# QK-normalised attention with a maxout feed-forward layer: the values' bound by a product with ones, SyncE's order by hand, weighted sums a slot later

## The chip, the cores and the metric

The kernel runs on one core of one Trainium2 chip. The metric is the device time in microseconds of one execution; lower is better. The compute engines are TensorE (PE in the profile, its weight loads PEld), VectorE (DVE), ScalarE (ACT) and GpSimd (POOL). SyncE (SP) issues every DMA of this kernel from one queue, in order.

## The reference

```python
# q, k, v: (8, 12, 448, 64)   g_q, g_k: (64,)
q_n = q / sqrt(mean(q*q, -1) + 1e-6) * g_q        # k_n likewise with g_k
scores = matmul(q_n, k_n^T) / sqrt(64)
attn = exp(scores - max(scores)); attn = attn / (sum(attn) + 1e-9)
x = matmul(attn, v)                               # heads side by side: (3584, 768)
h = maximum(maximum(x @ w1, x @ w2), x @ w3)      # each w: (768, 768) float64
out = h @ w_out                                   # float32 (3584, 768)
```

The four weight matrices come in as float64 and are decoded to float32 by integer operations on the chip. Products run at nearly float32 accuracy: queries, keys, attention weights and values are split into a float16 head and a float16 remainder, feed-forward operands into two float32r parts, and three of the four cross products are summed.

## The kernel before, in words

Work goes by pairs of heads, 48 pairs (8 batches of 6); a pair is `g`. Its life is spread over several turns of the main loop:

- Three pairs ahead, `load_k` and `load_q` fetch rows. `load_kv` uses four DMAs for a pair: for each of the two heads the first 384 rows, three to a partition, and the last 64 on one half of the partitions. The rows lie in one of three fixed tiles, of which a strip was set to zero once.
- Two pairs ahead, `squares`, `inv_rms` and `scale_k` or `scale_q` normalise the rows (VectorE sums, GpSimd raises to the power -0.5 and multiplies).
- One pair ahead, `turn_k` and `turn_q` (both through `turn_rows`) split them into float16 parts (cast L251 on ScalarE, remainder L252 on GpSimd) and turn them with one DMA transpose each (L256). The parts' tiles `kp` and `qp` have two buffers. `load_v` fetches the values and `bound_v` finds a bound for their size: VectorE takes the largest magnitude of each partition (`most`), SyncE writes these 128 numbers to DRAM (`vscr`, L276) and reads them back to all partitions (`every`, L278), and `prep_v` reduces them to one number and splits the values by it (`vp`).
- In its own turn the pair's queries come in four chunks of 112. `scores` runs six matmuls per chunk into a two-bank tile `sc` of PSUM (two buffers). `softmax` takes the negated row maximum (L326), scales it (L327) and runs the exponential with its row sum (L333). `weights` turns the sum into a factor (L343, L347), makes the float16 head (L350, ScalarE) and remainder (L351, VectorE) of the weights, and turns both with a DMA transpose into `pt` (L357).
- One pair later, `add_values` sums the weighted values in seven steps; step 3 (L372) is for the two half blocks of 64 keys, the others are at L378. `fold` brings a head's sum to its place, `finish` splits it for the feed-forward part.

The feed-forward part of a batch is a generator, `ffn`, taken in thirds. A third is three matmuls. Layer 1 (L439) has 18 units of six thirds, one per weight block; `split_w` casts and splits the block of the next unit (L112 on ScalarE, L113 on GpSimd) at a unit's second third, and `fetch` (L415, tile `wf`, two buffers) loads the block of the unit after that at its third. Layer 2 (L483) has 42 thirds on the mean and loads nothing. The decoding of the weights (`prep_w`: load `raw`, five VectorE instructions, store to DRAM as `wscr`; `prep_wo` likewise for `w_out`, kept on chip) goes beside the first nine pairs, by the table `DECODES`.

A turn of the main loop has eight slots, `i` = 0 to 7. In each slot three thirds of the feed-forward part are taken (a fourth when two batches wait). Scores of chunks 0 and 1 stand in slot 0, of chunks 2 and 3 in slot 4; the weights of the four chunks in slots 1, 2, 5 and 6; the seven steps of the weighted sums of the pair before in slots 1 to 7.

What sets the order: only TensorE's instructions stay in the order of the program text. All other queues, SyncE's included, are ordered by a planner that models the run when the program is built; at run time each queue is worked off in order, and a waiting instruction holds all behind it.

```python
ctx.enter_context(tc.manual_schedule(engines={mybir.EngineType.PE}))
```

Of the kernel before, what the change touches and what calls it, by code (L numbers as in the profile page):

```python
# [7 lines left out]
F32 = mybir.dt.float32  # L8
# [9 lines left out]
P = 128  # L18
# [18 lines left out]
def qknorm_attention_maxout_ffn_kernel(  # L37
# [60 lines left out]
    HALVES = (slice(0, 64), slice(64, 128))  # L98

    kv_rows = {}  # L100
    for name in ("kr", "vr"):
        kv_rows[name] = [const.tile([P, 2, 4, D], F32, name=f"{name}{i}") for i in range(3)]
        for t in kv_rows[name]:
            nc.gpsimd.memset(t[HALVES[1], 0, 3], 0.0)
            nc.gpsimd.memset(t[HALVES[0], 1, 0], 0.0)

# [68 lines left out]

    def load_kv(g, name, src):
        b, pr = divmod(g, NP)
        t = kv_rows[name][g % 3]
        for h in range(2):
            rows = src[b, 2 * pr + h]  # L180
            nc.sync.dma_start(
                out=t[:, h, h:h + 3],
                in_=rows[0:3 * P].rearrange("(p c) d -> p c d", c=3),
            )
            nc.sync.dma_start(out=t[HALVES[h], h, 3 - 3 * h], in_=rows[3 * P:S])
        st.setdefault(g, {})[name] = t
# [8 lines left out]
    def squares(g, what):  # L195
        s = st[g]
        src, rows = (s["kr"], P) if what == "k" else (s["qr"], QP)
        src = src.rearrange("p h c d -> p (h c) d")
        sq = sb.tile([P, 8, D], F32, name="sq", tag="rows", bufs=2)
        if g < EARLY:  # L200
            nc.scalar.activation(sq[:rows], src, AF.Square)
        else:
            nc.gpsimd.tensor_tensor(out=sq[:rows], in0=src, in1=src, op=ALU.mult)
        s["sq"] = sq[:rows]

    def inv_rms(g):
        s = st[g]
        sq = s.pop("sq")
        rows = sq.shape[0]
        ss = sb.tile([P, 8], F32, name="ss", tag="ss", bufs=2)  # L210
        nc.vector.tensor_reduce(ss[:rows], sq, axis=AX, op=ALU.add)
        nc.vector.tensor_scalar(  # L212
            out=ss[:rows], in0=ss[:rows], scalar1=1.0 / D / QK_UP ** 2,
            scalar2=RMS_EPS / QK_UP ** 2, op0=ALU.mult, op1=ALU.add,
        )
        ri = sb.tile([P, 8], F32, name="ri", tag="ri", bufs=2)
        nc.gpsimd.tensor_tensor(  # L217
            out=ri[:rows], in0=ss[:rows], in1=half_neg[:rows], op=ALU.pow
        )
        s["ri"] = ri  # L220

    def scale_rows(g, what, rows):
        s = st[g]
        r, ri = s.pop(what + "r"), s.pop("ri")
        n = sb.tile([rows, 4, 2, D], F32, name=what + "n", tag="rows", bufs=2)
        nc.gpsimd.tensor_tensor(
            out=n.rearrange("p c h d -> p h c d"),
            in0=r,
            in1=ri[:rows].rearrange("p (h c o) -> p h c o", h=2, o=1).broadcast_to([rows, 2, 4, D]),
            op=ALU.mult,  # L230
        )
        s[what + "n"] = n

    def scale_q(g):
        scale_rows(g, "q", QP)
        n = st[g]["qn"].rearrange("p c h d -> p (c h) d")
# [4 lines left out]
        )  # L241

    def scale_k(g):
        scale_rows(g, "k", P)


    def turn_rows(g, what, rows):
        s = st[g]
        n = s.pop(what + "n").rearrange("p c h d -> p (c h d)")
        parts = sb.tile([rows, 2, 4 * P], F16, name=what + "p", bufs=2)  # L250
# [3 lines left out]
        )  # L254
        t = sb.tile([P, 2, 4, rows], F16, name=what + "t", bufs=2)
# [6 lines left out]
    def turn_q(g):  # L262
        turn_rows(g, "q", QP)

    def turn_k(g):
        turn_rows(g, "k", P)


    def bound_v(g):
        s = st[g]  # L270
        most = sb.tile([P, 1], F32, name="most", bufs=2)
        nc.vector.tensor_reduce(
            most, s["vr"].rearrange("p h c d -> p (h c d)"), axis=AX, op=ALU.max, apply_absolute_value=True
        )
# [3 lines left out]
        nc.sync.dma_start(  # L278
            out=every, in_=scr.rearrange("(o p) -> o p", o=1).broadcast_to([P, P])
        )  # L280
        s["every"] = every


    def prep_v(g):
        s = st[g]
        vr, every = s.pop("vr").rearrange("p h c d -> p (h c) d"), s.pop("every")
# [11 lines left out]
        vp = sb.tile([P, 8, 2, D], F16, name="vp", bufs=2)  # L298
# [11 lines left out]
    def scores(g, chunks):  # L310
        s = st[g]
        qt, kt = s["qs"], s["ks"].rearrange("p a c r -> p a (c r)")
        for c in chunks:
            sc = ps_s.tile([P, 2, 512], F32, name="sc", tag="s")
            for n, (qp, kp) in enumerate(TERMS):
# [5 lines left out]
            s["sc", c] = sc  # L321

    def softmax(g, c):
        sc = st[g].pop(("sc", c))
        nm = sb.tile([QP, 2], F32, name="nm", bufs=3)
# [228 lines left out]
    for g in range(2):  # L554
# [3 lines left out]
        if g == 0:  # L558
            turn_k(0)
# [103 lines left out]
```

## Time and profile before

| | |
|---|---|
| median of 3 runs | 1873.96 us (1869.73 to 1875.49) |
| the profiled execution | 1879.87 us, span of its instructions 1878.1 us |
| mean granted TensorE clock | 0.804 of full |
| DMA | 513958 packets, 231.80 MB, mean 123 GB/s |
| TensorE matmuls / VectorE / ScalarE / GpSimd instructions | 5520 / 1952 / 1760 / 726 |

The profile is of one execution. In its rows, `out<-in` names the tiles, `x` a count; `<-` behind idle time names what ended it. A duration next to a transfer is from its issue to its landing. SPq is SyncE's own queue.

### The profile page before, as it was taken

What the parts mean: (1) busy time and instruction counts of PE and PEld (TensorE: products, weight loads), DVE (VectorE), ACT (ScalarE), POOL (GpSimd) and SP (SyncE); (2) the same over time, 40 slices, a digit from 0 to 9 for tenths busy, and PEclk for the clock granted to TensorE, in tenths of its full rate; (3) what the DMA queues carried; (4) which work ended last, traced back from release to release, by engine and by line L of the source; (5) the groups of instructions that cost most, each with busy time, mean ns of one, the idle gap of its engine ahead of it and who ended that gap; (6) DMA issues with size and microseconds to landing.
All of it is one profiled execution on the core that took longest, in us unless ns stands there. A gap on an engine that the chain in (4) does not pass through costs nothing. (4 is left out here: it accounts for less than half of the span.)

```text
span 1878.1 us, 18561 instructions
## 1 busy us (share of the span) xinstructions
PE 1140.2 (61%) x5520; PEld 860.2 (46%) x5520; DVE 1185.7 (63%) x1952; ACT 873.7 (47%) x1760; POOL 982.3 (52%) x726
## 2 busy tenths in 40 slices
PE   1013214646675775677567666666767667678898
PEld 0001102424453554455455454545555445566798
DVE  4667879957665765677566676567675677466310
ACT  2334334445454544454544454554544555456331
POOL 5344445656644664466555575366655566334252
PEclk9966556869788787788778777887878778788999
DMA  7979867665546545666755664754856663555431
GB/s 119 171 152 148 175 159 156 138 121 114 126 91 145 126 95 117 119 124 107 133 122 106 128 134 93 130 130 95 159 110 116 132 128 90 119 123 129 94 103 58
DMA packets 513958, 231.80 MB, mean 123 GB/s; under 512 B 433472, under 2 KB 488768, under 8 KB 513856
## 3 DMA queue, kind: packets, MB, share of 16 engines
q1 hardware_dynamic: 513856, 230.60, 60.1%
q8 instruction: 44, 0.72, 0.2%
q14 instruction: 58, 0.48, 0.1%
HBM read 111.74 MB, written 18.11 MB: 69 GB/s over the span
## 5 line engine op out<-in xcount | busy, mean ns | idle before, releaser
L439 PE MATMUL acc<-xt,wt 128*128 128x448 f32 x2592 | 689.6, 412 | 158.9 <-ACT wt L112 102.5
L439 PEld LDWEIGHTS acc<-xt,wt 128*128 128x128 f32 x2592 | 533.1, 209 | 269.6 <-ACT wt L112 113.2
L351 DVE SCALAR_TENSOR_TENSOR pp<-p,rs,pp 112x448 f16<-112x448 f32 x384 | 421.9, 1134 | 249.1 <-ACT pp L350 236.9
L333 ACT ACTIVATE p<-sc,nm,down 112x448 f32<-112x448 f32 x384 | 273.9, 721 | 313.3 <-DVE nm L327 284.3
L378 PE MATMUL av<-pt,vp 128*128 128x448 f16 x576 | 181.8, 410 | 385.8 <-DMA pt<-pp 272.8
L113 POOL TENSOR_TENSOR wt<-wf,wt 128x768 fp32r<-128x768 f32 x144 | 272.0, 1889 | 232.3 <-ACT wt L112 231.3
L217 POOL TENSOR_TENSOR ri<-ss,half_neg 128x8 f32<-128x8 f32 x96 | 175.0, 1823 | 199.9 <-DVE ss L212 172.0
L350 ACT ACTIVATE pp<-p,rs 112x448 f16<-112x448 f32 x384 | 233.0, 663 | 58.8 <-issue 39.6
L378 PEld LDWEIGHTS <-vp 128*128 128x128 f16 x576 | 38.6, 105 | 461.0 <-issue 329.2
L483 PE MATMUL acc<-wo_sb,ht 128*128 128x384 f32 x864 | 200.4, 382 | 66.3 <-ACT osb L488 35.0
L317 PE MATMUL sc<-kt,qt 64*112 64x448 f16 x1152 | 157.7, 411 | 121.9 <-ACT p L333 91.3
L252 POOL TENSOR_TENSOR kp<-kn,kp 128x512 f16<-128x512 f32 x48 | 59.4, 1237 | 318.2 <-ACT kp L251 294.9
L483 PEld LDWEIGHTS acc<-wo_sb,ht 128*128 128x128 f32 x864 | 171.1, 212 | 85.0 <-ACT osb L488 37.3
L326 DVE TENSOR_REDUCE nm<-sc 112x2 f32<-112x896 f32 x192 | 204.5, 1078 | 4.1 <-PE sc L317 2.7
L112 ACT CAST wt<-wf 128x768 fp32r<-128x768 f32 x144 | 119.6, 831 | 128.3 <-PE acc L439 59.3
L317 PEld LDWEIGHTS <-qt 64*112 64x112 f16 x1152 | 85.4, 146 | 179.1 <-issue 102.3
L343 DVE TENSOR_SCALAR sm<-sm 112x2 f32<-112x2 f32 x192 | 72.5, 378 | 130.0 <-ACT p L333 129.7
L453 DVE TENSOR_TENSOR m<-acc,m 128x448 f32<-128x448 f32 x96 | 59.0, 615 | 114.8 <-PE acc L439 114.6
L251 ACT CAST kp<-kn 128x512 f16<-128x512 f32 x48 | 29.6, 616 | 195.6 <-DMA kt<-kp 191.2
L391 DVE SCALAR_TENSOR_TENSOR x<-av,vscale,x 64x448 f32<-64x448 f32 x96 | 65.2, 679 | 53.9 <-ACT x L390 52.6
L327 DVE TENSOR_SCALAR nm<-nm,down 112x2 f32<-112x2 f32 x192 | 90.8, 488 | 0.3
L390 ACT ACTIVATE x<-av,vscale 64x448 f32<-64x448 f32 x96 | 60.4, 630 | 56.6 <-PE av L372 49.5
(55 smaller groups left out, 1204.8 us busy)
## 6 DMA issues: line engine op xcount, KB each, us to landing
wf<-wscr SPq DMA_DIRECT2D x144, 384.0 KB, 3.8
raw<-in_moe_w_dram SPq DMA_DIRECT2D x18, 768.0 KB, 6.8
qr<-in_q_dram SPq DMA_DIRECT2D x48, 224.0 KB, 3.5
kr<-in_k_dram SPq DMA_DIRECT2D x96, 96.0 KB, 4.0
vr<-in_v_dram SPq DMA_DIRECT2D x96, 96.0 KB, 2.5
wscr<-d_f SPq DMA_DIRECT2D x18, 384.0 KB, 3.6
raw<-in_moe_w_out_dram SPq DMA_DIRECT2D x6, 768.0 KB, 5.5
every<-vscr SPq DMA_DIRECT2D x48, 64.0 KB, 4.9
```

Source lines behind the costliest of these rows:

```text
L112: nc.scalar.copy(dst_hi, src)
L113: nc.gpsimd.tensor_tensor(out=dst_lo, in0=src, in1=dst_hi.bitcast(F32), op=ALU.subtract)
L217: nc.gpsimd.tensor_tensor(out=ri[:rows], in0=ss[:rows], in1=half_neg[:rows], op=ALU.pow)
L317: nc.tensor.matmul(sc[:QP, h, :S], qt[rows, qp, c], kt[rows, kp, KEYS[h]], start=n == 0, stop=n == len(TERMS) - 1,)
L326: nc.vector.tensor_reduce(nm, sc[:QP, :, :S], axis=AX, op=ALU.max, negate=True)
L327: nc.vector.tensor_scalar(out=nm, in0=nm, scalar1=down[:QP], scalar2=None, op0=ALU.mult)
L333: nc.scalar.activation(p[:, h], sc[:QP, h, :S], AF.Exp, bias=nm[:, h:h + 1], scale=down[:QP], accum_out=sm[:, h:h + 1],)
L350: nc.scalar.activation(pp[:, 0, h], p[:, h], AF.Copy, scale=rs[:, h:h + 1])
L351: nc.vector.scalar_tensor_tensor(out=pp[:, 1, h], in0=p[:, h], scalar=rs[:, h:h + 1], in1=pp[:, 0, h], op0=ALU.mult, op1=ALU.subtract,)
L378: nc.tensor.matmul(s["av"][h][:, :S], vp[:, u + h], pt[:, 7 * part + u], start=u == 0 and part == 0, stop=u == 6 and part == 1,)
L439: nc.tensor.matmul(acc[:, :S], wt[:, wp, c], xs[c][:, xp], start=(c == 0 and n == 0), stop=(c == NCT - 1 and n == 2),)
L483: nc.tensor.matmul(acc[:, :HW], lhs, wo_sb[:, f, wp, half * HW:(half + 1) * HW], start=(f == 0 and n == 0), stop=(f == NFT - 1 and n == 2),)
```

## The change

- The values' bound: `largest_v` (VectorE, slot 7 of the pair before) keeps `most`; `bound_v` multiplies a 128x128 tile of ones with it on TensorE, which puts the sum of the 128 numbers on every partition, into one spare column of the scores' tile of chunk 2, in slot 4. The sum is a bound too. `prep_v` follows in slot 5 in place of 3. The DRAM trip, `every` and one reduction go.
- SyncE's instructions now also stay in the order of the text. For that the text is rearranged: `turn_rows` and `weights` are each cut in two, the computing (`part_rows`, `weights`) and the transposes (`turn_rows`, `turn_weights`), which stand at the end of a slot. Keys are parted in slot 1 and turned in slot 3, queries in 3 and 4. Decodings come ahead of a slot's loads and weights.
- Loads: three DMAs per pair for keys and as many for values, into tiles of seven blocks of 64 columns; the zero strip is kept in two fixed tiles `key_rows` behind the scaling, which now takes four GpSimd products. Values have seven blocks in place of eight.
- Weighted sums: the six whole steps stand in slots 2 to 7 in place of 1 to 7, and step 3 at the start of slot 0 of the next turn, followed there by both folds and `finish`.
- Small columns: the negated row maximum (`low`) and the row sums (`sm`) are written to spare columns of the scores' tile in PSUM, not to tiles of their own.

```diff
-    kv_rows = {}
...
+    ones = const.tile([P, P], F32, name="ones")
+    nc.vector.memset(ones, 1.0)
+    key_rows = [const.tile([P, 4, 2, D], F32, name=f"kn{i}") for i in range(2)]
...
     def load_kv(g, name, src):
+        t = sb.tile([P, 8, D], F32, name=name, bufs=2)
+        rows = src[b, 2 * pr:2 * pr + 2]
+        nc.sync.dma_start(
+            out=t.rearrange("p (h c) d -> p h c d", h=2)[:, :, 0:3],
+            in_=rows[:, 0:3 * P].rearrange("h (p c) d -> p h c d", c=3),
+        )
         for h in range(2):
+            nc.sync.dma_start(out=t[HALVES[h], 3], in_=rows[h, 3 * P:S])
...
     def scale_k(g):
+        for h, rows in enumerate(HALVES):
+            own = slice(4 * h, 4 * h + 3)
+            nc.gpsimd.tensor_tensor(
+                out=kn[:, h:h + 3, h], in0=kr[:, own],
+                in1=ri[:, own].broadcast_to([P, 3, D]), op=ALU.mult,
+            )
+            nc.gpsimd.tensor_tensor(
+                out=kn[rows, 3 - 3 * h, h:h + 1], in0=kr[rows, 3:4],
+                in1=ri[rows, 3:4].broadcast_to([64, 1, D]), op=ALU.mult,
+            )
...
-        scr = dram.tile([P], F32, name=f"vscr_{g}")
-        nc.sync.dma_start(out=scr.rearrange("(p o) -> p o", o=1), in_=most)
-        every = sb.tile([P, P], F32, name="every", bufs=2)
-        nc.sync.dma_start(
-            out=every, in_=scr.rearrange("(o p) -> o p", o=1).broadcast_to([P, P])
-        )
...
+    def bound_v(g, corner):
+        s = st[g]
+        nc.tensor.matmul(corner, ones, s.pop("most"), start=True, stop=True)
         scales = sb.tile([P, 3], F32, name="vscale", bufs=3)
-        nc.vector.tensor_reduce(scales[:, 0:1], every, axis=AX, op=ALU.max)
         nc.vector.tensor_scalar(
-            out=scales[:, 0:1], in0=scales[:, 0:1], scalar1=LEAST, scalar2=1.0 / V_UP,
+            out=scales[:, 0:1], in0=corner, scalar1=LEAST, scalar2=1.0 / V_UP,
             op0=ALU.max, op1=ALU.mult,
         )
...
-    def scores(g, chunks):
+    def scores(g, chunks, bound=None):
...
+        if bound is not None:
+            bound_v(bound, s["sc", chunks[0]][:, 0, S:S + 1])
...
+        low = sc[:QP, 0, S + 8:S + 10]
+        nc.vector.tensor_reduce(low, sc[:QP, :, :S], axis=AX, op=ALU.max, negate=True)
         nm = sb.tile([QP, 2], F32, name="nm", bufs=3)
-        nc.vector.tensor_reduce(nm, sc[:QP, :, :S], axis=AX, op=ALU.max, negate=True)
         nc.vector.tensor_scalar(
-            out=nm, in0=nm, scalar1=down[:QP], scalar2=None, op0=ALU.mult
+            out=nm, in0=low, scalar1=down[:QP], scalar2=None, op0=ALU.mult
         )
...
-        sm = sb.tile([QP, 2], F32, name="sm", bufs=3)
+        sm = sc[:QP, 1, S + 8:S + 10]
...
-    ctx.enter_context(tc.manual_schedule(engines={mybir.EngineType.PE}))
+    ctx.enter_context(
+        tc.manual_schedule(engines={mybir.EngineType.PE, mybir.EngineType.SP})
+    )
...
         for i in range(8):
-            if w >= 0 and i > 0:
-                add_values(w, i - 1)
+            if i == 0 and w > 0:
+                add_values(w - 1, 3)
+            if g < G and i == 0:
+                scores(g, (0, 1))
+            if g < G and i == 4:
+                scores(g, (2, 3), bound=g)
+            if w >= 0 and i > 1:
+                add_values(w, (0, 1, 2, 4, 5, 6)[i - 2])
             if g < G and i % 4 == 0:
-                scores(g, (i // 2, i // 2 + 1))
                 softmax(g, i // 2)
                 softmax(g, i // 2 + 1)
+            if i == 0 and w > 0:
+                fold(w - 1, 0)
+                fold(w - 1, 1)
+                finish(w - 1, x_of[(w - 1) // NP])
             ffn_third()
+            for _ in range(n_dec(g, i)):
+                decodes.pop(0)()
+            if g + 3 < G:
+                if i == 0:
+                    load_k(g + 3)
+                if i == 3:
+                    load_q(g + 3)
+            if g + 1 < G:
+                if i == 1:
+                    part_rows(g + 1, "k")
+                if i == 3:
+                    load_v(g + 1)
+                    part_rows(g + 1, "q")
+                if i == 7:
+                    largest_v(g + 1)
             if g < G and i % 4 in (1, 2):
                 weights(g, i // 4 * 2 + i % 4 - 1)
...
             ffn_third()
             if len(queue) > 1:
                 ffn_third()
+            if g < G and i % 4 in (1, 2):
+                turn_weights(g, i // 4 * 2 + i % 4 - 1)
+            if g + 1 < G:
+                if i == 3:
+                    turn_rows(g + 1, "k")
+                if i == 4:
+                    turn_rows(g + 1, "q")
```

More of the change, by code (lines that the diff above doesn't have):

```diff
@@ L98, in qknorm_attention_maxout_ffn_kernel @@
     HALVES = (slice(0, 64), slice(64, 128))
[L100 to L105 removed]
+    ones = const.tile([P, P], F32, name="ones")
+    nc.vector.memset(ones, 1.0)
+    key_rows = [const.tile([P, 4, 2, D], F32, name=f"kn{i}") for i in range(2)]
+    for t in key_rows:
+        nc.gpsimd.memset(t[HALVES[1], 3, 0], 0.0)
+        nc.gpsimd.memset(t[HALVES[0], 0, 1], 0.0)
     wo_sb = const.tile([P, NFT, 2, DO], F32R, name="wo_sb")
@@ L254, in turn_rows @@
         )
+        s[what + "p"] = parts
+    def turn_rows(g, what):
+        s = st[g]
+        parts = s.pop(what + "p")
+        rows = parts.shape[0]
         t = sb.tile([P, 2, 4, rows], F16, name=what + "t", bufs=2)
@@ L314, in scores @@
             sc = ps_s.tile([P, 2, 512], F32, name="sc", tag="s")
+            s["sc", c] = sc
+        if bound is not None:
+            bound_v(bound, s["sc", chunks[0]][:, 0, S:S + 1])
+        for c in chunks:
+            sc = s["sc", c]
             for n, (qp, kp) in enumerate(TERMS):
```

139 lines of the change are left out of this document (57 added, 82 removed).

## The prediction

> **What bounds the kernel now.** I read the page's head first, then the waits of the matmul engine in the stretch that holds most of the time, then the waits of SyncE's own queue, then one group in order of time.
>
> ```profile
> span 1878.1 us, 18561 instructions
> ...
> PE 1140.2 (61%) x5520; PEld 860.2 (46%) x5520; DVE 1185.7 (63%) x1952; ACT 873.7 (47%) x1760; POOL 982.3 (52%) x726
> ```
>
> No engine is near full, so the time is made by waits.
>
> Next, ScalarE's softmax exponentials (L333) counted in three stages. Columns: stretch, its length, busy time and count, granted TensorE clock, DMA share, GB/s. A head pair takes 16 of these instructions, so the count gives the pairs.
>
> ```profile
> 40.00:312.00 272.00, 42.63 (x113) 0.68 0.87 163
> 312.00:1729.50 1417.50, 237.21 (x641) 0.81 0.58 119
> 1645.40:1703.90 58.50, 11.87 (x32) 0.86 0.59 134
> 1729.50:1878.10 148.60, 6.08 (x16) 0.96 0.32 85
> ```
>
> So 272.0 us go to seven pairs with the weight decoding beside them, 1417.5 us to 40 pairs with the feed-forward part on TensorE (35.4 us each), 148.6 us to the last pair and the tail, and 40 us lie ahead. The middle stage decides. What TensorE waits for there (total, times, longest), and SyncE's queue:
>
> ```profile
> PE av L378 <- DMA pt<-pp: 148.5, 21, 17.6
> PE acc L439 <- ACT wt L112: 102.3, 26, 11.6
> PE av L378 <- issue: 86.2, 13, 17.7
> PE acc L439 <- POOL wt L113: 45.5, 35, 2.8
> ```
> ```profile
> SPq L278 <- DMA vscr<-most: 236.2, 35, 8.9
> SPq L357 <- DVE pp L351: 117.6, 35, 8.3
> ```
>
> TensorE waits for turned weights (av, L378; its "issue" rows stand at the same place) and for split feed-forward weights (wt). The largest wait of SyncE's queue is the return trip of the values' bound. One group in order of time shows a third wait behind both:
>
> ```profile
> 997.15 1.42 SPq L256 DMA_TRANSPOSE kt<-kp  x1
> ...
> 1000.99 0.62 ACT L251 CAST kp<-kn 128x512 f16<-128x512 f32 x1 [6.81 <-DMA kt<-kp]
> ...
> 1003.94 1.12 PE L439 MATMUL acc<-xt,wt 128*128 128x448 f32 x2 [7.24 <-ACT wt L112]
> ```
>
> The planner has put the keys' transpose so late in SyncE's order that the cast of the keys two pairs on, which needs the same buffer, stands at the head of ScalarE's queue for 6.81 us. The cast of the next feed-forward weights comes after it on that queue, and TensorE stands 7.24 us for those. In the middle stage this happens in nearly every pair:
>
> ```profile
> ACT kp L251 <- DMA kt<-kp: 177.1, 32, 8.7
> ```
>
> The 58.5 us row above is the control that the trace gives for nothing: those two pairs come after the last such cast and take 29.2 us each. What still stops TensorE there is the turned weights:
>
> ```profile
> 1670.74 1.46 SPq L357 DMA_TRANSPOSE pt<-pp  x1
> ...
> 1675.47 0.90 PE L378 MATMUL av<-pt,vp 128*128 128x448 f16 x2 [6.32 <-issue]
> ```
>
> **Part by part: the middle stage.** *Order by hand.* Keys are turned at the end of slot 3, queries at slot 4 of the pair before, and their casts stand at slots 1 and 3. The buffer that the next cast but one needs is then free a whole pair early: the 177.1 us go. *No DRAM trip.* The 236.2 us of SyncE's queue go, with two DMA issues per pair; six loads of keys and values stand in place of eight (about 0.5 us of queue each, like the two in the decoding rows below). *Weighted sums one slot later.* They get one more slot of matmuls as cover. TensorE's work at full rate, from the chain that ended last:
>
> ```profile
> 1735.48 0.40 PE av L378 x2
> 1735.87 1.80 PE acc L439 x9
> 1737.67 0.48 PE av L372 x4
> 1738.16 1.14 PE sc L317 x12
> ```
>
> A pair is 8 x 1.80 + 6 x 0.40 + 0.48 + 2 x 1.14 = 19.6 us, and a slot is 2.2 us. From the 29.2 us of the control I take off 2.2 for the slot.
>
> *Small columns in PSUM.* VectorE's scaling of the row maximum, nanoseconds (min/median/max), and below it the mean of the same instruction (after the busy time):
>
> ```profile
> L327 DVE TENSOR_SCALAR nm<-nm,down x192: 206/217/3196, 39.7 to 1744.0; 112x2 f32<-112x2 f32 x192
> ```
> ```profile
> L327 DVE TENSOR_SCALAR nm<-nm,down 112x2 f32<-112x2 f32 x192 | 90.8, 488 | 0.3
> ```
>
> The median of 217 against a mean of 488 says that a few are held up long. Whether a PSUM operand avoids that, the trace does not show. The gain on the way from scores to weights of a pair of chunks is between a loss of 0.2 us (an estimate: half the minimum again for each of two, if a PSUM access is that much slower) and 2 x 0.27 us; I take 0.5, since the mean lies so far above the median. The Trainium skill, page "SBUF — State Buffer", section "Who interferes with whom", says that such a tensor_scalar in SBUF can enter a two-port mode and then is shut out for a whole GpSimd instruction; the page "VectorE: DVE Perf Modes", section "Why PSUM operands drop a tier", says that a PSUM operand rules that mode out. By that rule the whole gap between mean and median goes for L327; without it nothing does, and the sum is 0.5 us per pair worse.
>
> *The product with ones.* It takes the place of a reduction, but TensorE now runs one matmul into a column of the scores' own tile, VectorE reads it, and the scores of chunks 2 and 3 follow into that bank. If they must wait for the read, everything behind them on TensorE's queue waits too: between 0.16 us (VectorE idle: a small instruction like L212 below) and 3.4 us (behind three weight remainders of 1.1, half of the pair of 2.13 below). I take 1.2, one such instruction, because VectorE is busy 63% of the time.
>
> So a pair without new trouble: 29.2 - 2.2 - 0.5 + 1.2 = 27.7 us. Four smaller GpSimd products for the keys in place of one are set against squares, powers and values over seven blocks in place of eight; GpSimd is busy 52% of the time and nothing on the way above waits for it: I take nothing, and if that cover were gone the three added instructions are the price.
>
> *What the hand order costs.* SyncE's queue now runs in program order. Turning the weights of chunk 0 stands at the end of slot 1 and waits for their remainder; behind it stand chunk 1's, the loads, both row transposes, and the fetches of feed-forward weights (wf) traced in slots 2 to 5. When are the remainders ready?
>
> ```profile
> 1007.10 2.49 PE L317 MATMUL sc<-kt,qt 64*112 64x448 f16 x12
> ```
> ```profile
> 1019.38 2.83 DVE L351 SCALAR_TENSOR_TENSOR pp<-p,rs,pp 112x448 f16<-112x448 f32 x2
> 1022.14 0.16 DVE L212 TENSOR_SCALAR ss<-ss 112x8 f32<-112x8 f32 x1
> 1022.21 2.13 DVE L351 SCALAR_TENSOR_TENSOR pp<-p,rs,pp 112x448 f16<-112x448 f32 x2
> ```
> ```profile
> L112 ACT CAST wt<-wf x144: 813/832/857, 119.7 to 1841.5; 128x768 fp32r<-128x768 f32 x144
> L113 POOL TENSOR_TENSOR wt<-wf,wt x144: 1795/1839/2469, 120.6 to 1842.4; 128x768 fp32r<-128x768 f32 x144
> ...
> DMA to landing us min/median/max: 2.8/3.8/15.2
> ```
>
> The scores end at 1009.6; chunk 0's remainder at 1022.2, 12.6 us later, chunk 1's at 1024.3. Put slot 0 at zero: scores end at 0.48 + 1.14 = 1.6, chunk 0's remainder (0.5 saved) at 13.7, its transpose leaves the queue 1.5 later (1.42 in the row above), the fetch behind it 0.5 later, lands after 3.8, and is cast (0.83) and split (1.84): 22.2. A fetch serves the unit that begins three slots later; for the one traced in slot 2 that is slot 5, which TensorE reaches at 3.4 + 1.8 + 2.2 + 2.2 + 3.3 = 12.9. It waits 9.3 us. For one traced in slot 3, with chunk 1's transpose ahead too, the difference is about the same. Fetches come every second slot, so each pair in the first layer has one such, and the later ones find TensorE late already. That pair takes 19.6 + 9.3 + 1.2 and some 1 us of second waits: 31 us; the scores-to-sums chain runs inside the wait. The second layer fetches nothing: 27.7. The first layer is 108 of 150 thirds of a batch, so the mean is 0.72 x 31 + 0.28 x 27.7 = 30.1, taken as 30: 40 x (35.4 - 30) = 217 us saved, with the stage's 1417.5 unrounded.
>
> **The decoding stage.** Here program order costs. Storing a decoded weight block now stands in the queue right behind its load, with the keys' load and all turned weights of the pair behind it:
>
> ```profile
> 22.40 0.59 SPq L150 DMA_DIRECT2D raw<-in_moe_w_dram  x1
> ...
> 37.03 0.53 SPq L156 DMA_DIRECT2D wscr<-d_f  x1
> ```
> ```profile
> raw<-in_moe_w_dram SPq DMA_DIRECT2D x18, 768.0 KB, 6.8
> ```
>
> From load to store took 14.6 us, at least the load's landing, 6.8. I take 13, near the upper end since five VectorE instructions have to lie between. Eighteen of them are 234 us; six transposes at 1.4 and seven loads at 0.5 per pair are 12 x 7 = 84; some 30 us of waits for weights between. 347 us in place of 272: +75 (between +30 and +140). The two pairs after it, with the last decodings beside the feed-forward part, get +20 as an estimate from the same 13 us.
>
> **Sum.** 1878.1 - 217 + 75 + 20 = 1756; the 40 us ahead and the tail of 148.6 keep their work. The profiled execution's own time is 1879.87, 1.8 more, and 0.3% above the median of 1873.96, so against the median about 1750. With 28.5 to 31.5 us per pair and the decoding bounds the case reaches from 1650 to 1870.
>
> **Rivals.**
> - *Late fetches are hidden* (SyncE keeps up because VectorE reaches the remainders sooner once nothing blocks ScalarE). For it: part of the 12.6 us is queueing. Against: the chain itself is long. Then 27.7 us everywhere: 1878.1 - 308 + 60 (decoding +40, and the 20) = 1630, about 1625.
> - *The read of the ones' product costs its upper bound* at every pair: 2.2 us more than I took, 48 times, 106: about 1855. The matmul of chunk 2 into that bank waits behind whatever VectorE has begun. The Trainium skill, page "PSUM — Partial Sum Buffer", section "PSUM bank collisions raise a hardware error", wants two engines kept apart on a bank, not merely on its columns; by it the wait is certain and only its size is open. No row of the trace shows this pair of accesses.
> - *Slower: the late fetch feeds back.* ScalarE's cast of wt waits at the head of its queue for the late wf, and exponentials and weights stand behind it, so SyncE's wait for the remainder grows and the next fetch is later still. Its place is the first layer's pairs; passed round once it adds some 6 us: 37 us there, 34.4 on the mean, 1878.1 - 40 + 95 = about 1930. It decides once a mean pair takes over 33.0 us (35.4 less 95 / 40), that is once TensorE's wait for wt in a first-layer pair passes 13 us in place of 9.3.
> - *The change doesn't do what it says*: ScalarE, VectorE and GpSimd stay in the planner's hands, and it may cast the keys so late that SyncE, in order, waits for them instead. About 1870, to either side.
>
> **How the numbers follow.** Forecast 0.47, fetches hidden 0.24, ones' product dear 0.10, feedback 0.13, no effect 0.06. Over 0.3% is what a measurement here tells from no change (1869.73 to 1875.49). Faster: 0.47 + 0.24 + 0.09 + 0.02 = 0.82; slower 0.13 + 0.02 = 0.15; the same 0.03. The range takes in the second case and most of the third: 1600 to 1870.
>
> **What would show it.** Right: no wait of the keys' cast for kt; none on vscr; 30 us per pair; TensorE's waits moved from av to wt, with SyncE's longest wait that for pp and a wf issue right behind it; a decoding stage longer than 272 us with SyncE waiting on d_f; L327's mean near its median. Wrong: pairs still over 33 us, a wait of TensorE for VectorE's column read ahead of the scores of over 2 us per pair, or a decoding stage as short as before.

## The result, and the profile after

| | before | after |
|---|---|---|
| median of 4 runs | 1871.85 us (1867.40 to 1875.49) | 1809.45 us (1800.15 to 1815.75) |
| the profiled execution, and its span | 1879.87, 1878.1 us | 1815.75, 1814.0 us |
| mean granted TensorE clock | 0.804 | 0.819 |

The ratio after to before is 0.9664, interval 0.9614 to 0.9713: 3.4% faster. Forecast were 1750 us, 6.6% faster. The direction was right and the time lies in the range, but only half of the gain came.

The head of the page after (span, then busy time, share and instructions of each engine):

```profile
span 1814.0 us, 18436 instructions
...
PE 1187.3 (65%) x5616; PEld 906.5 (50%) x5616; DVE 1112.6 (61%) x1905; ACT 866.7 (48%) x1760; POOL 1000.2 (55%) x862
```

As before, no engine is full. The same three stages after, counted by the exponentials (now L348; stretch, length, busy time and count, granted clock, DMA share, GB/s):

```profile
29.50:333.70 304.20, 43.50 (x112) 0.63 0.52 128
333.70:1666.10 1332.40, 232.90 (x641) 0.84 0.60 131
1666.10:1814.00 147.90, 5.85 (x16) 0.98 0.30 83
```

By stage, in us, from these rows and those of before:

| stage | before | after | moved | forecast |
|---|---|---|---|---|
| ahead of the first pair | 40.0 | 29.5 | -10.5 | 0 |
| seven pairs with decoding | 272.0 | 304.2 | +32.2 | +75 |
| forty pairs | 1417.5 | 1332.4 | -85.1 | -217 + 20 |
| last pair and tail | 148.6 | 147.9 | -0.7 | 0 |
| sum | 1878.1 | 1814.0 | -64.1 | -122 |

What SyncE's queue and ScalarE wait for in the forty pairs after (total, times, longest), one fence for each engine:

```profile
SPq L377 <- DVE pp L366: 472.3, 74, 20.9
```
```profile
ACT wt L112 <- DMA wf<-wscr: 159.2, 60, 9.5
...
ACT kp L261 <- DMA kt<-kp: 27.6, 13, 4.8
```

The keys' cast waits 27.6 us where it waited 177.1, and no wait on `vscr` exists. In their place SyncE's queue waits 472.3 us for the weights' remainders (117.6 before), and ScalarE 159.2 us for feed-forward weights that SyncE fetched late. One such fetch in order of time:

```profile
1079.99 1.24 SPq L272 DMA_TRANSPOSE qt<-qp  x1
...
1090.97 1.45 SPq L377 DMA_TRANSPOSE pt<-pp  x1
...
1092.52 0.94 SPq L434 DMA_DIRECT2D wf<-wscr  x1
...
1096.79 0.83 ACT L112 CAST wt<-wf 128x768 fp32r<-128x768 f32 x1 [4.86 <-DMA wf<-wscr]
...
1097.67 0.68 PE L458 MATMUL acc<-xt,wt 128*128 128x448 f32 x2 [0.59 <-ACT wt L112]
```

SyncE issues nothing from 1081.2 to 1091.0, because the turning of the weights at its head is not ready. The fetch behind it leaves at 1092.5, ScalarE stands 4.86 us for it, and TensorE 0.59 us behind that.

The stretch of 35 steady pairs by itself (g = 10 to 44, 561 exponentials in each; PE, PEld, DVE, ACT, POOL busy and count, granted clock, DMA share, GB/s), first before, then after, and then what TensorE waits for in it after:

```profile
441.80:1674.90 1233.10, 822.05 (x3972) 618.39 (x3970) 797.54 (x1319) 619.17 (x1261) 682.47 (x507) 0.80 0.59 119
```
```profile
475.70:1606.50 1130.80, 852.24 (x4064) 656.11 (x4064) 741.76 (x1292) 613.78 (x1264) 717.82 (x625) 0.85 0.60 130
```
```profile
PE acc L458 <- POOL wt L113: 76.0, 47, 4.0
PE acc L458 <- ACT wt L112: 59.4, 23, 5.4
PE sc L331 <- DVE vscale L292: 32.8, 35, 3.9
```

A steady pair went from 35.2 to 32.3 us; forecast were 30. It consists of TensorE's own work (852.24 / 35 = 24.3 us), of waits for `wt` (135.4 / 35 = 3.9), of the wait of the scores for VectorE's read of the ones' product (0.9) and of other waits (3.2; all waits of TensorE in this stretch are 280.7 us). The waits for `wt` did not grow: by the prediction's rows they came to (102.3 + 45.5) / 40 = 3.7 us per pair before; in the prediction's example they stood behind the keys' cast. What shrank are the waits of the weighted sums (`av`): 148.5 us for `pt` before, 14.3 after.

### The profile page after: what moved, and what is told of

The parts are those of the page before. It is cut to its first block, busy times and chain, and to the rows that moved or that the text cites. A ratio compares the mean times of both kernels' runs of the same rounds, so it can differ in the third digit from the quotient of the medians.

```text
span 1814.0 us, 18436 instructions
## 1 busy us (share of the span) xinstructions
PE 1187.3 (65%) x5616; PEld 906.5 (50%) x5616; DVE 1112.6 (61%) x1905; ACT 866.7 (48%) x1760; POOL 1000.2 (55%) x862
## 4 chain that ended last, share of the span: by engine, by line
DVE 28%; DMA 20%; PE 13%; SPq 10%; issue 10%; ACT 9%; POOL 9%; ACTq 0%; POOLq 0%; DVEq 0%
DVE pp L366 12%; PE acc L458 7%; DMA wf<-wscr 7%; DMA raw<-in_moe_w_dram 4%; PE acc L502 4%; DVE raw L124 3%; ACT p L348 3%; DVE sc L340 3%; ACT pp L365 3%; SPq L377 3%; POOL wt L113 3%; DMA vr<-in_v_dram 3%; DMA kr<-in_k_dram 2%; SPq L186 2%; SPq L170 2%
## 5 line engine op out<-in xcount | busy, mean ns | idle before, releaser
L458 PE MATMUL acc<-xt,wt 128*128 128x448 f32 x2592 | 705.4, 419 | 215.0 <-POOL wt L113 101.7
L331 PE MATMUL sc<-kt,qt 64*112 64x448 f16 x1152 | 174.0, 444 | 281.4 <-DMA qt<-qp 214.8
L348 ACT ACTIVATE p<-sc,nm,down 112x448 f32<-112x448 f32 x384 | 269.6, 731 | 170.2 <-DVE nm L342 158.5
L331 PEld LDWEIGHTS <-qt 64*112 64x112 f16 x1152 | 105.6, 158 | 322.6 <-DMA qt<-qp 222.6
L218 POOL TENSOR_TENSOR ri<-ss,half_neg 128x7 f32<-128x7 f32 x96 | 159.8, 1665 | 177.8 <-DVE ss L213 139.7
L340 DVE TENSOR_REDUCE sc<-sc 112x2 f32<-112x896 f32 x192 | 206.2, 1092 | 37.2 <-PE sc L331 35.5
L204 POOL TENSOR_TENSOR sq<-qr 112x512 f32<-112x512 f32 x40 | 43.0, 1075 | 138.9 <-DMA qr<-in_q_dram 138.8
L204 POOL TENSOR_TENSOR sq<-kr 128x448 f32<-128x448 f32 x40 | 38.3, 958 | 142.7 <-DMA kr<-in_k_dram 132.0
L212 DVE TENSOR_REDUCE ss<-sq 128x7 f32<-128x448 f32 x96 | 62.0, 646 | 85.5 <-POOL sq L204 71.3
L283 DVE TENSOR_REDUCE most<-vr 128x1 f32<-128x448 f32 x48 | 29.7, 618 | 122.1 <-DMA vr<-in_v_dram 122.1
L124 DVE TENSOR_SCALAR raw<-raw 128x768 int16<-128x768 int16 (+1 forms) x48 | 66.1, 1377 | 52.0 <-DMA raw<-in_moe_w_dram 48.0
```

What stands on the lines that cost most here:

```text
L124: nc.vector.tensor_scalar(out=top, in0=top, scalar1=float(least), scalar2=None, op0=ALU.max)
L218: nc.gpsimd.tensor_tensor(out=ri, in0=ss, in1=half_neg[:rows, :n], op=ALU.pow)
L331: nc.tensor.matmul(sc[:QP, h, :S], qt[rows, qp, c], kt[rows, kp, KEYS[h]], start=n == 0, stop=n == len(TERMS) - 1,)
L340: nc.vector.tensor_reduce(low, sc[:QP, :, :S], axis=AX, op=ALU.max, negate=True)
L348: nc.scalar.activation(p[:, h], sc[:QP, h, :S], AF.Exp, bias=nm[:, h:h + 1], scale=down[:QP], accum_out=sm[:, h:h + 1],)
L458: nc.tensor.matmul(acc[:, :S], wt[:, wp, c], xs[c][:, xp], start=(c == 0 and n == 0), stop=(c == NCT - 1 and n == 2),)
```

## Experiments

The experiments' chips ran the kernel before in about 1829 us, so kernels are compared by their ratio to the kernel before on the same chip. The change itself was timed only on another chip, where the kernel before took 1871.85 us; it is at 0.966 there. Differences from 0.966 take this ratio to carry over, which no run shows, and may be off by a point or two; those among the other kernels do not depend on it.

| kernel | ratio | interval |
|---|---|---|
| a_wf3: the change, fetches one unit earlier | 0.933 | 0.930 to 0.937 |
| a_store: the change, decoded blocks stored later | 0.947 | 0.944 to 0.951 |
| a_plan: the change, SyncE ordered by the planner | 0.870 | 0.866 to 0.874 |
| b_kp3: before, a third buffer for keys and queries | 1.007 | 1.004 to 1.010 |
| p_dram: a_plan with the DRAM trip | 0.969 | 0.967 to 0.972 |
| p_av: a_plan, weighted sums in the old slots | 0.891 | 0.888 to 0.893 |
| p_small: a_plan, small columns in SBUF | 0.879 | 0.876 to 0.882 |
| p_corner: a_plan, ones' product behind the scores | 0.832 | 0.830 to 0.834 |
| b_ones: before with the ones' product alone | 0.910 | 0.907 to 0.912 |
| a_dram: the change with the DRAM trip | 1.214 | 1.210 to 1.218 |
| p_wf3_corner: p_corner, fetches one unit earlier | 0.834 | 0.831 to 0.837 |
| h_all3: the change, early fetch, late store, product behind | 0.850 | 0.847 to 0.853 |

### The late fetch: a_wf3

```diff
-            wf = sb.tile([P, NCT * P], F32, name="wf", bufs=2)
+            wf = sb.tile([P, NCT * P], F32, name="wf", bufs=3)
...
-                fetch(unit + 2)
+                fetch(unit + 3)
...
-                fetch(1)
+                fetch(2)
```

Room for the third buffer comes from `xt`, 11 buffers in place of 12.

> The changed kernel with the feed-forward weight blocks fetched one unit earlier (three wf buffers in place of two, one xt buffer given up for the space). Late-fetch theory (SyncE's hand order holds the fetches behind the turned weights): TensorE's wait for wt, 180 us between 300 and 1700 us in the changed kernel, falls below 80, a pair of the steady part goes from 32.3 us to about 28.5, and the time to about 1660 us. Rival, the chain from scores to turned weights is as long anyway: the waits move to the weighted sums and the scores, a pair stays over 31 us, the time over 1760.

Measured: 1704.14 us, 0.933; a steady pair takes 29.7 us. Waits of TensorE from 300 to 1500 us:

```profile
PE sc L331 <- DMA qt<-qp: 69.4, 19, 36.8
PE av L397 <- DMA pt<-pp: 67.5, 22, 7.8
PE sc L331 <- DVE vscale L292: 64.2, 38, 9.3
PE acc L458 <- POOL wt L113: 38.9, 24, 5.4
```

With an earlier fetch the `wt` waits shrink (in the 35 steady pairs from 135.4 to 39.2 us), and the kernel gains some 3.3 points. The late fetch is thus a cost of the hand order. TensorE now stands instead for turned weights and, less, for turned queries, which come through the same queue; 36.8 us of the `qt` row are a single wait that still lies in the decoding stage.

### The order by hand: a_plan

```diff
-        tc.manual_schedule(engines={mybir.EngineType.PE, mybir.EngineType.SP})
+        tc.manual_schedule(engines={mybir.EngineType.PE})
```

> The changed kernel with SyncE's order given back to the planner; everything else stays. If the hand order is what freed the keys' cast, ScalarE's wait for kt returns to over 100 us in the steady part; if the DRAM trip was what pushed the transposes late, it stays gone. Late-fetch theory: SyncE's wait for pp falls from 490 us towards the 118 of before and TensorE's wait for wt with it; the decoding stage gets back to about 272 us. Time by the first, 1800 to 1870; by the second, about 1700.

Measured: 1591.52 us, 0.870. The hand order costs some 9.6 points of the time before. Waits from 300 to 1500 us, ScalarE, then TensorE, then SyncE's queue:

```profile
ACT kp L261 <- DMA kt<-kp: 27.0, 16, 5.4
```
```profile
PE sc L331 <- DVE vscale L292: 91.9, 40, 7.5
```
```profile
SPq L377 <- DVE pp L366: 236.1, 67, 8.6
```

The first row broke the prediction's account: the wait of the keys' cast stays away (27.0 us) although the planner orders SyncE again, so the hand order was not needed for that. The wait for the ones' product grows, to 2.3 us at each pair. The decoding stage takes 195.2 us in place of 304.2:

```profile
41.40:236.60 195.20, 43.71 (x113) 0.67 0.77 193
```

### More buffers for the keys: b_kp3

```diff
-        parts = sb.tile([rows, 2, 4 * P], F16, name=what + "p", bufs=2)
+        parts = sb.tile([rows, 2, 4 * P], F16, name=what + "p", bufs=3)
```

Again `xt` has 11 buffers.

> The kernel before with three buffers in place of two for the split keys and queries (one xt buffer given up for the space), nothing else. Theory of the prediction: the cast no longer waits for the transpose of two pairs before, 177 us of ScalarE's queue go, a pair goes from 35.4 to 30 us or a little above, and the time to about 1680. Rival: the stall is slack that another wait takes over (turned weights, the DRAM trip in SyncE's queue), a pair stays above 33.5 and the time above 1800.

Measured: 1841.66 us, 1.007, no gain. From 300 to 1500 us, ScalarE and SyncE's queue:

```profile
ACT kp L251 <- DMA kt<-kp: 128.0, 31, 8.0
```
```profile
SPq L278 <- DMA vscr<-most: 185.5, 30, 8.2
```

The cast still waits, 31 times. With one buffer more the transpose still comes too late for the cast. The number of buffers is not what makes it late.

### The store of a decoded block: a_store

```diff
-        scr = dram.tile([P, NCT * P], F32, name=f"wscr_{ft}_{j}")
-        nc.sync.dma_start(out=scr, in_=f)
-        w_scr[ft, j] = scr
+        late.append([2, ft, j, f])
...
+    def store_w():
+        for s in late:
+            s[0] -= 1
+        while late and late[0][0] < 0:
+            _, ft, j, f = late.pop(0)
+            scr = dram.tile([P, NCT * P], F32, name=f"wscr_{ft}_{j}")
+            nc.sync.dma_start(out=scr, in_=f)
+            w_scr[ft, j] = scr
...
                 turn_weights(g, i // 4 * 2 + i % 4 - 1)
+            store_w()
```

The store leaves two slots after its load, behind that slot's turned weights.

> The changed kernel with the store of a decoded weight block put two slots later in SyncE's order, so that the queue need not stand while VectorE decodes. Theory: SyncE's 180 us of waits at the store before 334 us go, and the decoding stage, 304 us for the first seven pairs, gets back to 272 or less: about 1765 us. Rival: VectorE or the transfers set that stage and it stays within 10 us: about 1800.

Measured: 1731.03 us, 0.947, a gain of 1.9 points from 0.966. The decoding stage, first here, then in a_wf3, which stores as the change does and ran on the same chip (stretch, length, busy time and count of the exponentials, granted clock, DMA share, GB/s):

```profile
28.60:272.00 243.40, 43.27 (x113) 0.65 0.67 164
```
```profile
28.90:331.40 302.50, 43.48 (x112) 0.62 0.53 131
```

243.4 us in place of 302.5 there and 304.2 in the change; a steady pair stays at 32.1 us. So storing in program order is a second cost of the hand order, and it lies in this stage and the three pairs behind it (131.3 us, against 138.4 in a_wf3). The 59 us of this stage are 3.2% of 1829 us, more than the 1.9 points: on this chip the change seems to stand nearer to 0.98 than to 0.966 (an estimate), and the gains counted from 0.966 are then too small.

### The trip through DRAM: p_dram, a_dram and b_ones

The trip was put back into the change, once with SyncE planned (p_dram) and once in the hand order (a_dram). The rest of the change stays; `bound_v` then stands in slot 5 and reads `every`.

```diff
+        scr = dram.tile([P], F32, name=f"vscr_{g}")
+        nc.sync.dma_start(out=scr.rearrange("(p o) -> p o", o=1), in_=s.pop("most"))
+        s["every"] = sb.tile([P, P], F32, name="every", bufs=2)
+        nc.sync.dma_start(
+            out=s["every"], in_=scr.rearrange("(o p) -> o p", o=1).broadcast_to([P, P])
+        )
...
-        nc.tensor.matmul(corner, ones, s.pop("most"), start=True, stop=True)
+        nc.vector.tensor_reduce(scales[:, 0:1], s.pop("every"), axis=AX, op=ALU.max)
```

> The changed kernel with SyncE's order left to the planner (0.870 of the time before), and in it the values' bound by way of DRAM again. If the trip's wait in SyncE's queue is what pushed the transposes and so the keys' cast late, ScalarE's wait for kt returns (over 100 us between 300 and 1500 us, 27 without the trip), and the ratio to the kernel before rises to 0.95 or more. If the trip was hidden, the ratio stays within 0.01 of 0.870.

> The changed kernel, hand order kept, with the values' bound by way of DRAM again. If the hand order is a cost whatever else is there, the ratio is over 1.0, since SyncE now waits in order for the trip too. If the hand order cures what the trip does to the planner, the ratio stays at or below the 0.969 of the planned kernel with the trip.

The kernel b_ones is the kernel before with nothing but the product with ones, placed behind the scores of chunk 2, with `prep_v` there:

```diff
-        every = sb.tile([P, P], F32, name="every", bufs=2)
...
+            if c == 2:
+                s["corner"] = sc[:, 0, S:S + 1]
+                nc.tensor.matmul(s["corner"], ones, s.pop("most"), start=True, stop=True)
+                prep_v(g)
```

> The kernel before with one edit: the values' bound by the ones' product (behind the scores of chunk 2, so that no matmul follows into the bank), no DRAM trip; SyncE planned, weighted sums, loads and small columns as before. Theory: the trip is what pushes the transposes late in the planner's order, so ScalarE's wait for kt (177 us before) falls below 50 without touching the order, and the ratio is about 0.88. Rival: the other edits of the change are needed for that (keys parted and turned at other slots); the wait stays over 100 us and the ratio over 0.94.

Measured: p_dram 1774.62 us (0.969), a_dram 2217.82 us (1.214), b_ones 1662.73 us (0.910). From 300 to 1400 us in p_dram, ScalarE and SyncE's queue:

```profile
ACT kp L261 <- DMA kt<-kp: 196.5, 31, 10.6
```
```profile
SPq L290 <- DMA vscr<-most: 205.5, 31, 8.7
```

And in b_ones, ScalarE:

```profile
ACT kp L253 <- DMA kt<-kp: 31.2, 20, 3.9
```

This settles the keys' wait in a planned order. It comes back with the trip (196.5 us, 31 times) and goes with the product alone (31.2 us), and the planner makes the order in both. So the trip of 128 numbers by way of DRAM, whose return holds SyncE's queue for 205.5 / 31 = 6.6 us each time, makes the keys' transpose late there. How the planner comes to that place was not looked into.

In the hand order the trip costs far more. From 300 to 1400 us in a_dram (some 25 pairs), ScalarE, GpSimd, VectorE and SyncE's queue:

```profile
ACT kp L261 <- DMA kt<-kp: 28.3, 12, 11.5
```
```profile
POOL sq L204 <- DMA kr<-in_k_dram: 320.1, 26, 35.2
```
```profile
DVE vscale L297 <- DMA every<-vscr: 303.3, 25, 19.0
```
```profile
SPq L381 <- DVE pp L370: 284.4, 41, 17.8
SPq L290 <- DMA vscr<-most: 193.6, 25, 9.4
```

The keys' cast waits little (28.3 us) although the trip is there: the hand order ends that wait too, as the prediction said. But the loads of the next keys and the return of the bound now stand behind the weights, and GpSimd and VectorE wait for them far longer. The two parts of the change together:

| | DRAM trip | product with ones |
|---|---|---|
| SyncE planned | 0.969 | 0.870 |
| SyncE by hand | 1.214 | 0.966 |

The product is worth 9.9 points with SyncE planned and some 24.8 by hand. The hand order costs in both columns, 24.5 points with the trip.

### Slots and columns: p_av and p_small

Both are made from a_plan. In p_av the seven steps stand again in slots 1 to 7 of the pair's next turn, with the folds as before; in p_small the row maxima and sums have tiles of their own again.

```diff
-            if i == 0 and w > 0:
-                add_values(w - 1, 3)
...
+            if w >= 0 and i > 0:
+                add_values(w, i - 1)
...
-            if w >= 0 and i > 1:
-                add_values(w, (0, 1, 2, 4, 5, 6)[i - 2])
```

> The same planned kernel with the weighted sums in their old slots. By the prediction's term a slot is worth 2.2 us of 48 pairs, some 100 us: ratio 0.92, and TensorE's wait of the sums for pt rises from 44 us to over 120. Rival: something else ends the pair and the ratio stays under 0.885.

```diff
-        low = sc[:QP, 0, S + 8:S + 10]
+        low = sb.tile([QP, 2], F32, name="low", bufs=3)
...
-        sm = sc[:QP, 1, S + 8:S + 10]
+        sm = sb.tile([QP, 2], F32, name="sm", bufs=3)
```

> The same planned kernel with the row maxima and sums in tiles of their own in SBUF, as before the change. By the prediction 0.5 us a pair, 24 us: ratio 0.883, and the mean of the maximum's scaling back from about 220 to about 480 ns. If only one operand's place does nothing against GpSimd, the mean stays and the ratio too.

Measured: p_av 1627.48 us (0.891), p_small 1606.20 us (0.879). The later slot is worth 2.0 points, but not where it was looked for (a_plan is at 0.870). Without it TensorE waits again for turned weights (300 to 1400 us in p_av), yet a steady pair takes 29.5 us either way; the loss lies in the decoding stage (220.0 us against 195.2) and in the tail (149.4 against 143.8).

```profile
PE av L397 <- DMA pt<-pp: 115.9, 23, 9.9
```

The scaling of the row maximum, one instruction, after (PSUM operand) and in p_small (SBUF operand), nanoseconds min/median/max:

```profile
L342 DVE TENSOR_SCALAR nm<-sc,down x192: 196/210/222, 28.9 to 1677.2; 112x2 f32<-112x2 f32 x192
```
```profile
L342 DVE TENSOR_SCALAR nm<-low,down x192: 186/229/4082, 41.4 to 1469.2; 112x2 f32<-112x2 f32 x192
```

The tail of the distribution goes with the PSUM operand (in a_plan, planned like p_small, the longest is 222 ns as well). With it the time is 0.9 points lower, but again not in a steady pair, which takes 29.5 us with either: in the profiles the decoding stage and the three pairs behind it are longer in p_small, 198.9 and 135.7 us against 195.2 and 129.2.

### The place of the ones' product: p_corner

From a_plan; the product goes behind the scores of chunks 2 and 3 and into the tile of chunk 3.

```diff
-        if bound is not None:
-            bound_v(bound, s["sc", chunks[0]][:, 0, S:S + 1])
         for c in chunks:
...
+        if bound is not None:
+            bound_v(bound, s["sc", chunks[1]][:, 0, S:S + 1])
```

> The same planned kernel with the ones' product behind the scores of chunks 2 and 3, in chunk 3's tile, so that no matmul follows it into the bank. TensorE waited 92 us (40 times) for the column's reader ahead of the scores. If that wait was on the way, the ratio falls by about 0.03 to 0.84; if another wait takes it over, it stays at 0.87.

Measured: 1521.28 us, 0.832, the fastest kernel here. A steady pair takes 27.3 us. From 300 to 1400 us, ScalarE:

```profile
ACT p L348 <- DVE vscale L296: 74.3, 18, 7.0
...
ACT p L348 <- DVE vscale L292: 55.7, 18, 6.2
```

The wait has moved rather than gone: now the exponentials wait for VectorE's use of the bound, and TensorE's scores do not. The 2.3 us per pair of a_plan's row are what a steady pair gains (29.5 to 27.3).

### Do the repairs add up: p_wf3_corner and h_all3

The first is p_corner with a_wf3's edit, the second the change in its hand order with the edits of a_wf3, a_store and p_corner.

> The changed kernel with SyncE planned, the ones' product behind the scores, and the feed-forward weights fetched one unit earlier (one xt buffer given up). TensorE waited 70 us for wt in the version without the early fetch (ratio 0.832). If those waits are on the way, 0.81; if the planner had fetched early enough, 0.83 to 0.84.

> The changed kernel, hand order kept, with its three waits taken away together: wf fetched one unit earlier, the decoded block stored two slots later, the ones' product behind the scores. If these three are what the hand order and the product cost, the gains add up (0.033, 0.019 and 0.039 from the separate runs): ratio 0.875. If SyncE's wait for the weights' remainder bounds the pair in itself, it stays over 0.90.

Measured: 1523.31 us (0.834, its interval overlaps that of p_corner) and 1552.30 us (0.850). With SyncE planned the earlier fetch gains nothing. In the hand order the three repairs together gain 11.6 points, where a_wf3, a_store and p_corner's gain of 3.9 points add up to 9.1; the 0.966 enters the first sum once and the second twice. Against p_corner, which has the product in the same place, the hand order of SyncE then costs 1.8 points in place of some 9.6: most of its cost lay in the places of two DMAs, the fetch and the store. What is left lies in the decoding stage (245.4 us in h_all3 against 204.4 in p_corner); a steady pair takes 27.6 us against 27.3.

## Why the prediction was half right

**The gain in a steady pair: right in sign, too large.** Forecast were 30.0 us, measured 32.3. Term by term, mean over both layers, with 0.72 of the pairs in the first:

| term | forecast | measured |
|---|---|---|
| TensorE's own work | 19.6 | 24.3 |
| late fetch, waits for `wt` | 0.72 x 9.3 = 6.7 | 3.9 |
| read of the ones' product | 1.2 | 0.9 |
| other waits | 0.72 x 1 + 0.28 x (27.7 - 19.6 - 1.2) = 2.7 | 3.2 |
| sum | 30.2 | 32.3 |

The mis-sized term is "a pair is 8 x 1.80 + 6 x 0.40 + 0.48 + 2 x 1.14 = 19.6 us". Those durations come from the last stage, where the granted clock is 0.96. In the stage they were used for it is 0.80 before and 0.85 after, and TensorE's busy time there was 822.05 / 35 = 23.5 us per pair already before. By the clocks alone (an estimate) 19.6 x 0.96 / 0.80 = 23.5. The count is short too: 150 / 6 = 25 thirds fall to a pair, and 8 x 3 = 24 were counted (0.6 us). After, the busy time is 24.3 us although the clock is higher; 0.3 of it are the ones' product (11.2 us in the 35 pairs), and the rest of that rise is open. The stage's own busy time is the number to take. The 29.2 us control held it right (43.85 / 2 = 21.9 us busy, at a clock of 0.86); the first layer's 31 us was built on the other base. The step then also over-sized the late fetch: with TensorE slower it reaches the unit at 12.9 x 24.3 / 19.6 = 16.0 us in place of 12.9, and 22.2 less 16.0 is 6.2 (an estimate); measured were 3.9 / 0.72 = 5.4 per pair of the first layer.

**The late fetch: right as a mechanism.** The order of the queue, the 9.7 us of idle SyncE ahead of the remainder's transpose and the fetch right behind it are in the trace, and a_wf3 shows that they cost some 3.3 points. The rival that late fetches are hidden falls.

**"Order by hand ... the 177.1 us go": the wait went, but it was priced to the wrong edit.** The prediction took the hand order for the cure of the late transpose and gave the DRAM trip's 236.2 us of queue no price of their own in the sum. The wait is large only where the planner orders SyncE and the trip is there (177.1 us before, 196.5 in p_dram). The hand order ends it with the trip (28.3 in a_dram), and the loss of the trip ends it under the planner (27.0 in a_plan, 31.2 in b_ones). The step that failed is the reading of two waits of SyncE's queue as independent. The control of 29.2 us could not part them: in its two pairs the trip was made only once. SyncE's queue there, from 1645.4 to 1703.9 us before:

```profile
SPq L278 <- DMA vscr<-most: 7.3, 1, 7.3
```

So the forecast came within 60 us of the result partly by luck: it priced the hand order as a gain for the pairs, where a_plan shows that it costs some 9.6 points, and left the trip at nothing, where b_ones shows 9.0.

**The decoding stage: right mechanism, over-sized.** Forecast +75, measured +32. SyncE's waits ahead of the stores, from 29.5 to 333.7 us after, and one load and its store in order of time:

```profile
SPq L156 <- DVE d_f L137: 103.7, 9, 12.2
SPq L156 <- DVE rs L359: 50.8, 5, 10.5
SPq L156 <- DVE nm L342: 14.4, 1, 14.4
SPq L156 <- DVE rs L362: 11.9, 1, 11.9
```
```profile
129.25 0.57 SPq L150 DMA_DIRECT2D raw<-in_moe_w_dram  x1
141.97 0.34 SPq L156 DMA_DIRECT2D wscr<-d_f  x1
```

From load to store 12.7 us, against 13 taken. But it was 16 blocks in this stage, not 18, at 180.8 / 16 = 11.3 us of waiting: 181 us, not 234, and the rest came to 123 us for 114. The two blocks left over fall into the two pairs that follow, which took 111.0 us against 83.7: +27, forecast +20. The third pair won 15 us back. Against the planned order, 195.2 us in a_plan, the hand order costs over 100 us here (302.5 in a_wf3, on the same chip). The sum set it against the 272.0 of before, as if the rest of the change did nothing in this stage; with SyncE planned the rest of it takes the stage to 195.2.

**The ones' product.** 1.2 us per pair taken, 0.9 to 1.1 measured after, with a wait at every pair: TensorE's row has 35 waits in 35 steady pairs, and it is gone in p_corner, where the scores stand ahead of the product. The Trainium skill's page "PSUM — Partial Sum Buffer", section "PSUM bank collisions raise a hardware error", wants two engines kept apart by bank and not by address; the trace agrees as far as it goes, since the scores wait although they do not write the column that VectorE reads. But the price is not fixed: it is 2.3 us once other waits are gone (a_plan). The rival's 3.4 us at every pair were reached in neither kernel.

**Weighted sums a slot later.** 2.2 us per steady pair taken; nothing measured there with SyncE planned, 2.0 points from the stages at the two ends. In the hand order it was not tried alone.

**Small columns.** The group after (busy time, mean ns of one, idle time before):

```profile
L342 DVE TENSOR_SCALAR nm<-sc,down 112x2 f32<-112x2 f32 x192 | 37.2, 212 | 1.4
```

The mean is 212 ns, against 488 before. By the Trainium skill's page "SBUF — State Buffer", section "Who interferes with whom", as the prediction read it, the whole gap between mean and median was to go; the trace agrees (median 210). That GpSimd held the instruction up was not tried by itself. Against a_plan the 0.9 points are 16 us, or 0.3 us if spread over all pairs, near the 0.5 taken; but the steady pair did not change, so the term was right in size at best by luck.

**The other rivals.** The feedback of the late fetch did not decide: 5.4 us of waiting for `wt` in a first-layer pair, where 13 were its point. That the order has no effect falls with a_plan. **Ahead of the first pair** nothing was forecast; the 10.5 us gained there go with the hand order (29.5, 28.9 and 28.6 us in the hand-ordered kernels after, a_wf3 and a_store, 41.4 in a_plan), though the planned b_ones starts at 31.6 too.

## What to carry to other kernels

Take the work of the bounding engine from the busy time of the stage in question, not from durations of a stage with another granted clock. A DMA that waits for another DMA in a queue that is worked off in order costs everything placed behind it, so look for a way on the engines first, and price the waits that follow it together with it. If a queue is ordered by hand, walk through it once more for each instruction whose operand is made just ahead of it, and put what others wait for, loads above all, in front of it.

## What the runs showed of the hardware

The granted clock is higher where TensorE stands less: in the 35 steady pairs it is 0.80 before (TensorE busy 822.05 of 1233.10 us, 67%) and 0.85 after (75%). In a_plan and p_corner it is 0.88 (77%) and 0.92 (83%), the third figure from the end of their rows:

```profile
365.80:1398.60 1032.80, 799.06 (x4055) 630.80 (x4053) 765.23 (x1281) 608.51 (x1261) 686.81 (x597) 0.88 0.64 140
```
```profile
369.20:1324.00 954.80, 789.31 (x4056) 605.95 (x4054) 722.19 (x1282) 605.76 (x1261) 686.09 (x600) 0.92 0.70 151
```

The matmuls took 24.3 us per pair after, 22.8 in a_plan and 22.6 in p_corner. So a wait that is removed can be paid back more than once: p_corner's steady pair gained 2.2 us on a_plan's, of which 0.3 are TensorE's own busy time. The busy time does not follow the clock alone, though: at 0.80, before, it was 23.5 us, less than after. The Trainium skill, page "TensorE: Matmul & The Clock Gate", section "Part 1: The HAM clock gate (the "warmup" mystery)", says that the clock is held back by default and released by activity; the four rows of the clock agree in direction, and no run here varied the activity alone.

The smallest transfer was among the slowest. Transfers of the kernel before (count, KB each, median us from issue to landing):

```profile
wf<-wscr SPq DMA_DIRECT2D x144, 384.0 KB, 3.8
...
vscr<-most SPq DMA_DIRECT2D x48, 0.5 KB, 8.1
```

Writing half a kilobyte from 128 partitions took 8.1 us, twice as long as loading 384 KB; that is the wait that stood in SyncE's queue.

A single small instruction can be held for long: the scaling of two columns took up to 4082 ns with an SBUF operand in p_small and at most 222 ns with a PSUM operand in a_plan.
